# Four banks for the transposes of the first batch, five loads cut at 98 partitions, and one score bank masked by GpSimd

## The chip, the cores and the metric

The kernel runs on one core of a Trainium2 chip. Five engines take part, each with its own queue of instructions that it works through in order: TensorE (PE in the profile) multiplies matrices, VectorE (DVE), ScalarE (ACT) and GpSimd (POOL) work elementwise, and SyncE (SP) issues the transfers between memory and the on-chip buffers. They wait for each other by semaphores. Sixteen DMA engines move the bytes. TensorE writes its results into eight banks of PSUM, each 128 partitions of 512 float32 values; the other engines copy them out.

The metric is device time in microseconds, the median of several runs. A profile shows one execution: its span runs from the first to the last recorded instruction, and its device time is a little longer.

## The reference

Two layers follow each other, for four batches, 8 heads, 768 positions and heads of 48 columns.

```python
state = 0                                       # per batch and head, 48 x 48
for t in range(768):
    state = alpha[:, :, t, :, None] * state + outer(k[:, :, t], v[:, :, t])
    y[:, :, t] = q[:, :, t] @ state
x = y with the heads side by side               # batch, 768, 384
h = relu(x^T @ w_tok1) @ w_tok2                 # mixes the 768 positions, 256 wide
u = x + h^T
out = u + relu(u @ w_ch1) @ w_ch2               # mixes the 384 columns, 1536 wide
```

The first layer is a linear attention with a decay per column, the second a mixer with a token part and a channel part. Inputs and outputs are float32.

## The kernel before, in words

The recurrence is cut into chunks of 128 positions. Inside a chunk the decay is taken out by prefix sums of log alpha: ScalarE takes the logarithm (`la`, line 243), TensorE sums it with a triangular matrix (`cum`), ScalarE takes the exponentials of the sum with both signs (`ek`, `eq`, lines 256 and 258), and k and q are multiplied by them (`pkk`, `pkq`, line 275). TensorE transposes both, multiplies them to scores (`gt`, line 521 in the first batch), a mask keeps the causal half of the scores (`gm`, line 309), and the masked scores times v, together with the state so far, give y (`y`, `inter`), which is copied to `x` (line 333). The state itself goes from chunk to chunk (`state`, `id`, `ss`).

The chunks of batch 0 are worked in three pairs of chunks (256 positions, even and odd positions apart). For a pair there are two transposes of k and two of q, each of four 128x128 blocks. Before the change, one bank holds both transposes of k and another both transposes of q (line 472). Two copies empty each bank, one for each half: `tpk` (line 479) into `tk`, `tpq` (line 481) into `tq`. The half of `tpk` is the half of one transpose. The half of `tpq` takes columns of both transposes, since it interleaves even and odd positions again. Copies of one bank by two engines are ordered one behind the other. The score product of a pair comes in two parts (one for each s), each into two banks, and reads half of `tk` and all of `tq`.

The mixer of batch 0 follows: token products (`tok1`, line 582, one for each chunk and half of w_tok1), `ht` (line 589 or 591), then `xt` and `uT` (lines 629 and 634) that put u transposed into banks, copies `ut` (line 640), and the two channel products `ch1` (line 691, a relu copy `rt` behind each) and `ch2` (line 715, an output copy `o`, line 725 or 728, behind the last). The channel products of a batch are far more work on TensorE than the rest, and they are laid between the chunks of the next batches.

Loads come by SP in the order of the string `LOADS`: `a0 k0 q0 a1 k1 q1 a2 v0 k2 q2 v1 v2 t0 t1 t2 t3 m0 m1`. The letters a, k, q, v with a number are the inputs of one pair of chunks of batch 0 (384 KB). t0 and t1 are the halves of w_tok1, t2 and t3 those of w_tok2 (384 KB each), m0 and m1 the halves of w_ch1 (1152 KB each). n0 to n3, quarters of w_ch2 (576 KB each), come among the loads of batch 1 (string `SECOND`). All weights arrive in float32 and are cast to bf16 (`cast`, lines 756 and 762). Each transfer signals one of eight semaphores in turn, and SP issues the ninth when the first has landed.

The order of the work is written out by hand in the string `ORDER`: every token is one operation by its number in the list `g.ops`, with the engine that does it where there is a choice (A, D or P for ScalarE, VectorE or GpSimd) and, behind the point, the banks that it opens. `f3` is a fill: a matmul on zeros into bank 3 (line 792), which computes nothing that is used. Every engine gets its operations in this order. Nothing at run time changes it.

Of the kernel before, what the change touches and what calls it, by code (L numbers as in the profile page):

```python
# [17 lines left out]
FUSE = 99  # L18
FETCH, BLOCK, AHEAD, ARRIVES = 193, 256, 449, (4.5, 30.0, 3.0)
# [6 lines left out]
0 1 f0 2 f0 f0 f0 f0 f0 3 f0 f0 f0 f0 f0 4 28 f0 29 f0 f0 30.0 5 31.1 32 f2 f2 38 6 f2 35 f2 33 f2 f2 f2 39 f2 34 f2  # L26
36 40 f2 43.2 41 7 f3 66 47.3 f4 65 48 44 49A 50D f4 67.4 46A 45D 68.5 69 f6 51.67 75 72 54.01 8 70 52 f3 f3 76 f3 73
f3 77 f3 80.3 78 f2 9 84.2 56 f6 85 105 81 71 f6 104 87D f6 f6 10 86A f6 f6 83D 106.6 82A 55 107.5 108 53 91.14 11 114
88.23 92 f0 42P 37A f0 f0 109 90 f0 58.07 115 89 57.13 60A 93 f2 116 12 f2 f2 59 f2 f2 f2 112 f2 111 63 61 117 14
123.2 64A f0 62 f0 124 74A 79P 119.0 110 16 120 125D 126A f4 94.41 122A 121D 18 96 127.57 97 130.36 95.20 128 113A  # L30
118P 100 132 98 102 133.4 99A 20 131 13P f5 103A 169.5 101 163.6 24 166.2 f3 15P 129 141.3 135 142.0 143 136 134.17
17P 137 139 145 138D 147 140A 144 146 259 148 150 149 151 19D 152 172.4 178.1 162A 161D 175.7 f0 173 176 174A 167 177D
260 164 168A 170 22D 21P 165A 179 f0 171A 23D f0 261 f0 180A f0 189.0 201.3 190A 195.4 262 202A 181.7 27D 25P 196A
185.2 26D 182A 153 193.6 186A 211.5 264 194D 223.1 263 212D 227.0 224A 265.3 228A 266.4 155 267 217.7 273 270 207.2
274 209.6 268 300 208D 218A 276 213.5 210D 215.1 214A 269 187.0 301 271 216A 203.4 188A 219.3 275 204A 302 225.2 220A
154D 199.7 272 226A 278.65 277 279 200A 303 221.1 280D 281A 156P 183.0 222A 282 283 184A 292.43 284D 285A 197.2 304
294 286.71 157 305 198D 289.05 205.6 287 306.4 288 206A 159 191.2 308 291 307.7 309 311 239.6 296 314 343 290 315
249.1 297 192D 293.54 344 312 319.37 298 295A 345 254.0 316 299A 234.2 158A 346 317 244.5 347 310 313 160D 240 318 348
245 351 241 349 320 352.4 242A 321D 246 322A 354 235 247D 353 350 358 236 356 243 323 362 324 237D 333.64 357 325A
326D 376.5 238 363.2 335 250 248 355 364 336 486 365 327.37 251 487 329 366 367 330.62 328 252A 488 255 332 368 256  # L40
339 369 359.73 331 257A 370.12 340 229.4 361A 360D 253 372D 371A 377 373.60 258 510 334.73 375 489 381.21 341 490 374
337 230 342A 378 382 338A 491 379.5 383 231 380A 492 384.0 232D 511.6 385A 493 513 388.3 512 516 233 386.2 389A 514
517 494 521 495 515 387D 522.7 390.1 496 523 398.5 391 524 394.4 526 396.0 399 392.6 395 400.3 527 535.2 393 518.17
401 497 402.54 528 519A 397 529.63 525 403A 553.1 404D 498 520A 536 405.05 530A 416.4 499 554 406A 440.7 407D 555 531A
500 417D 420.2 539 434.6 421D 441A 501 532.10 435A 550.53 534 422.4 502 430.2 551 546 423A 540.7 533 431A 452.6 558
552 442.0 541 537.5 453D 503 542 438.4 544 538D 559.2 439A 556.1 443D 504 560 543 412.3 545 557D 561 426.6 413D 505
432.7 564 427A 410.5 506 433A 446.4 562 411A 565 408.0 507 447A 563 572.1 577 450.2 409D 508 454.3 573 451A 547.67 574
455D 566.54 509 548A 578.0 549D 591.1 568A 567D 448.2 720 592 580 424.3 584 449D 579 588.76 583 721 425A 569.54 590
418.1 596 582 436.2 570 419A 414.0 571 437A 581 597.3 593 589 722 610.6 575.5 598 444.1 415D 599 601 723 576A 594.2
611 445A 481.4 595D 602 724 744 428.7 476.0 600 429A 725 603 604.35 612 585.61 605A 726 466.2 587D 586A 477 727 606A  # L50
482 728 607.73 751 615.16 609 483 729 755 616 471.5 608 478 617 613.3 730 479 472 614A 484 618.1 480 762 456.7 619D
473 485 773 622.6 731 474 732 620.0 623A 475 457 621A 733 458 734 634.3 459 630.4 735 628.1 635 632.5 631 624.6 780
460 626.0 629 461.7 625 792 736 627 462 737 633 463 636.34 738 464 639.16 637A 467 638D 640A 641D 465 468 799 774.0
469 745.5 775 793.7 656.4 746 778 747 756.3 470 650.6 795 739 757 749 684.1 651D 740 758 644.2 685D 776 748 662.5 794
760 645D 741 660.6 811 663D 657A 678.3 750 742 661D 787.0 769.1 679A 812.7 770 759 668.2 743 777 813 761 672.5 788 814
664.4 669A 673D 789 670.6 665A 666.3 779 671A 646.1 830 667D 682.0 798 647A 831.7 683A 806.2 781.54 797 832 807 763.63
833 752.10 765D 658.2 783A 835 754D 764A 674.7 753D 659D 782A 686.3 808 675D 800.40 687A 803.16 796 802D 816 784.25
801A 766.73 804 680.0 768 818 654.4 681A 836 767 648.1 655A 844.3 786 642.0 649A 817 771.7 785 822.41 643A 652.5 772A
805 834 837 790.2 824 815 653A 809.0 791A 823 838.76 810A 819.51 825.2 839D 820A 828.4 840D 676.0 821A 826 715.7 829D
827 677A 849.65 841.21 845 716 843 846 700.4 851 695.0 850 696 842 852.3 688.1 853D 847.5 689A 705.6 848D 697 854.2  # L60
698 699 717 855A 710.3 718 711 701 719 702 856.1 703 704 712 857A 690.5 713 858.0 714 868.2 859 862.7 860.4 869 864.1
863 866.3 691 861 867 692 865 706 693 873.02 694 870.74 874A 875D 707 871D 872A 910.3 708 894.1 911A 709 880.5 895A
908.2 881D 906.0 909A 912.7 907A 900.4 913A 876.6 901A 896.3 877A 918.1 897A 914.5 919D 904.2 915A 922.0 905D 902.7
923D 920.4 903A 898.6 921A 916.3 899A 888.1 917A 890.5 889A 884.2 891D 878.0 885A 886.7 879A 882.4 887A 892.6 883D
929.3 893A 939.1 930 931 940 932 944.5 933 945 946 934.2 947 941 948 924.0 942 925 943 926 935 927 936 928 949.7 937
950 938 951 954.4 955 952 956 953 957 958
# [12 lines left out]
class Graph:  # L79
# [5 lines left out]
    def add(self, name, costs, emit, reads=(), writes=(), prio=0, dma=None, new=(), tail=0.0, rows=False, loose=False, n=0, late=0.0):  # L85
        self.ops.append(Op(costs, emit, new))
        return self.ops[-1]
# [6 lines left out]
def kernel(  # L94
# [12 lines left out]
    nc = tc.nc  # L107
# [73 lines left out]
    gm_t = many("gm", 2 * NG, [128, 4, 128])  # L181
    ss_t = many("ss", NSS, [128, H, D])
    x_t = many("x", NX, [128, HD])
    ht_t = many("ht", 2 * NDT, [128, HD])
# [19 lines left out]
    def load_input(dst, src, service, keys, prio, loose=False):  # L204
        return g.add("load", {"SP": 0.06}, lambda e: nc.sync.dma_start(dst, src), writes=keys, prio=prio, dma=service, loose=loose)  # L205
# [629 lines left out]
```

## Time and profile before

| | |
|---|---|
| device time, median of 3 runs | 174.05 us (174.0 to 175.09) |
| device time of the profiled execution | 174.24 us |
| its span | 172.5 us |
| TensorE busy | 166.5 us (96%) |
| VectorE busy | 102.0 us (59%) |
| ScalarE busy | 96.0 us (56%) |
| GpSimd busy | 72.3 us (42%) |
| fills of line 792 | 61, 15.1 us |
| loads and stores | 30.2 MB, 175 GB/s over the span |
| granted TensorE clock | 1.00 throughout |

TensorE's busy time counts matmuls that overlap as one stretch, and it counts the fills: a busy TensorE is not always one that does useful work. The lines of the profile have the form start, duration, engine, line, operation, output <- inputs. A bracket at the end tells how long the engine sat idle before it and what it waited for. Tile names leave numbers out: `bank` is any of the eight banks.

### The profile page before, as it was taken

What the parts mean: (1) busy time and instruction counts of PE and PEld (TensorE: products, weight loads), DVE (VectorE), ACT (ScalarE), POOL (GpSimd) and SP (SyncE); (2) the same over time, 40 slices, a digit from 0 to 9 for tenths busy, and PEclk for the clock granted to TensorE, in tenths of its full rate; (3) what the DMA queues carried; (4) which work ended last, traced back from release to release, by engine and by line L of the source; (5) the groups of instructions that cost most, each with busy time, mean ns of one, the idle gap of its engine ahead of it and who ended that gap; (6) DMA issues with size and microseconds to landing.
All of it is one profiled execution on the core that took longest, in us unless ns stands there. A gap on an engine that the chain in (4) does not pass through costs nothing.

```text
span 172.5 us, 5143 instructions
## 1 busy us (share of the span) xinstructions
PE 166.5 (96%) x2099; PEld 106.8 (62%) x2099; DVE 102.0 (59%) x212; ACT 96.0 (56%) x206; POOL 72.3 (42%) x114
## 2 busy tenths in 40 slices
PE   7999979999999999999999999999999999999993
PEld 3566656665666567566666665666676656656562
DVE  3159977544653597689593727495988248132231
ACT  2577552699865655497887231699771112865000
POOL 7252542319485782944877111499941000000000
PEclk9999999999999999999999999999999999999999
DMA  5999999999998999999999999995000221100133
GB/s 134 261 261 265 232 335 398 309 234 337 256 307 168 205 254 219 225 170 198 165 204 151 196 219 223 211 210 92 4 4 0 79 104 50 46 4 0 46 115 113
DMA packets 86150, 30.20 MB, mean 175 GB/s; under 512 B 79600, under 2 KB 85104, under 8 KB 86128
## 3 DMA queue, kind: packets, MB, share of 16 engines
q1 hardware_dynamic: 86128, 29.89, 75.2%
q8 instruction: 16, 0.26, 0.7%
q14 instruction: 6, 0.05, 0.1%
HBM read 25.17 MB, written 4.72 MB: 173 GB/s over the span
## 4 chain that ended last, share of the span: by engine, by line
PE 78%; DVE 6%; POOL 4%; DMA 3%; issue 3%; ACT 2%; SPq 1%; DVEq 0%; POOLq 0%
PE bank L691 27%; PE bank L715 23%; PE bank L289 4%; PE bank L651 3%; DMA ina<-in_alpha_dram 3%; PE bank L602 3%; DVE gm L309 2%; PE bank L387 2%; PE bank L338 2%; PE bank L423 2%; POOL pkk L275 2%; PE bank L521 1%; PE bank L411 1%; PE bank L352 1%; SPq L205 1%
## 5 line engine op out<-in xcount | busy, mean ns | idle before, releaser
L691 PE MATMUL bank<-ut,wc 128*128 128x384 bf16 x288 | 51.1, 326 | 0.0
L691 PEld LDWEIGHTS <-wc 128*128 128x128 bf16 x288 | 26.6, 98 | 16.5
L275 POOL TENSOR_TENSOR pkk<-ink,ek 128x384 bf16<-128x384 f32 x24 | 24.3, 1022 | 17.7 <-ACT ek L256 14.9
L715 PE MATMUL bank<-wc,rt 128*128 128x384 bf16 x144 | 26.5, 326 | 0.0
L715 PE MATMUL bank<-wc,rt_late 128*128 128x384 bf16 (+2 forms) x156 | 25.1, 314 | 0.0
L728 DVE TENSOR_TENSOR o<-bank,x 128x384 f32<-128x384 f32 (+2 forms) x19 | 10.1, 536 | 18.2 <-PE bank L715 18.2
L589 ACT ACTIVATE rt<-bank 128x384 bf16<-128x384 f32 x33 | 16.3, 494 | 7.4 <-PE bank L691 7.0
L282 POOL CAST vb<-inv 128x384 bf16<-128x384 f32 x21 | 10.5, 506 | 22.3 <-DMA inv<-in_v_dram 17.6
L715 PEld LDWEIGHTS <-rt_late 128*128 128x128 bf16 x156 | 14.4, 98 | 8.2
L275 POOL TENSOR_TENSOR pkq<-inq,eq 128x384 bf16<-128x384 f32 x18 | 17.9, 1003 | 2.8 <-ACT eq L258 2.8
L589 ACT ACTIVATE rt_late<-bank 128x384 bf16<-128x384 f32 x33 | 16.1, 495 | 5.3 <-PE bank L691 5.3
L309 DVE TENSOR_TENSOR gm<-bank,u 128x512 bf16<-128x512 f32 x28 | 17.3, 682 | 2.8 <-PE bank L387 2.6
L243 ACT ACTIVATE la<-ina 128x384 bf16<-128x384 f32 x24 | 12.1, 526 | 10.8 <-DMA ina<-in_alpha_dram 10.8
L715 PEld LDWEIGHTS <-rt 128*128 128x128 bf16 x144 | 13.2, 98 | 7.7
L792 PE MATMUL bank<-zeros 128*128 128x384 bf16 x61 | 15.1, 372 | 1.4 <-DVE la L192 1.2
L591 DVE TENSOR_SCALAR rt_late<-bank 128x384 bf16<-128x384 f32 x15 | 8.3, 554 | 10.0 <-PE bank L691 8.3
L309 DVE TENSOR_TENSOR gm<-bank,pmask 128x512 bf16<-128x512 f32 x20 | 12.7, 682 | 1.4 <-PE bank L521 1.3
L256 ACT ACTIVATE ek<-bank 128x384 f32<-128x384 f32 x24 | 11.4, 498 | 3.5 <-PE bank L355 2.0
L333 ACT CAST x<-bank 128x384 bf16<-128x384 f32 x16 | 7.3, 483 | 10.6 <-PE bank L338 9.4
L322 POOL TENSOR_TENSOR ss<-st,al 128x384 bf16<-128x384 f32 x12 | 10.0, 832 | 7.4 <-DVE st L319 5.4
L591 DVE TENSOR_SCALAR rt<-bank 128x384 bf16<-128x384 f32 x15 | 7.9, 554 | 5.3 <-PE bank L691 5.3
L297 ACT COPY tkq<-bank 128x512 bf16<-128x512 bf16 x17 | 9.3, 602 | 2.8 <-PE bank L289 2.7
(118 smaller groups left out, 237.3 us busy)
## 6 DMA issues: line engine op xcount, KB each, us to landing
out_dram<-o SPq DMA_DIRECT2D x23, 192.0 KB, 2.6
ina<-in_alpha_dram SPq DMA_DIRECT2D x14, 192.0 KB, 4.3
ink<-in_k_dram SPq DMA_DIRECT2D x14, 192.0 KB, 4.6
inq<-in_q_dram SPq DMA_DIRECT2D x14, 192.0 KB, 4.5
inv<-in_v_dram SPq DMA_DIRECT2D x14, 192.0 KB, 4.4
rt_late<-in_moe_w_ch_dram SPq DMA_DIRECT2D x2, 1152.0 KB, 10.1
rt_late<-in_moe_w_ch_dram SPq DMA_DIRECT2D x4, 576.0 KB, 7.1
ina<-in_alpha_dram SPq DMA_DIRECT2D x5, 384.0 KB, 6.3
```

What stands on the lines that cost most here:

```text
L243: g.add("la", {"ACT": 0.43}, lambda e: act.activation(la[:, :, 0:D], t, AF.Ln), key, [u["la"][1]], pr + 5)
L256: g.add("ek", {"ACT": 0.38}, lambda e: act.activation(ek, banks[bank.place][:, 0:HD], AF.Exp, scale=-1.0), [bank], [kek], pr + 4)
L275: lambda e, dst=dst, src=src, ex=ex: {"POOL": gps, "DVE": dve}[e].tensor_tensor(dst[:, :, 0:D], src, ex().rearrange("p (h d) -> p h d", h= ...
L282: lambda e: evict[e](vb, src), ksrc, [u["vb"][1]], pr + 4)
L309: g.add("gm", {"DVE": 0.60}, lambda e: dve.tensor_tensor(gm, banks[bank.place].rearrange("p (j t) -> p j t", j=4), wide(mask, [[0, 4], lis ...
L322: g.add("ss", {"POOL": 0.79}, lambda e: gps.tensor_tensor(ss, st.rearrange("p (h d) -> p h d", h=H), wide(al, [[1, 8], [0, D]]), ALU.mult) ...
L589: act.activation(dst, src, AF.Relu)
L591: dve.tensor_scalar_max(dst, src, 0.0)
L691: pe.matmul(banks[bank.place][:, 0:HD], lhsT=wc1[wp][:, kc, off : off + 128], rhs=ut_t[b % 2][:, kc, cs], start=(kc == 0), stop=(kc == NM ...
L715: pe.matmul(banks[bank.place][:, 0 : hi - lo], lhsT=rt_t[(b * NDC + mc) % NRT][:, i * 128 : i * 128 + 128], rhs=wc2[:, mc, lo:hi], start=( ...
L728: g.add("o", {"DVE": 0.09 + 0.38 * width}, lambda e, i=i, bank=bank, o=o, lo=lo, hi=hi: dve.tensor_tensor(o[:, lo:hi], banks[bank.place][: ...
L792: pe.matmul(banks[place][:, 0:HD], lhsT=zeros[:, 0:128], rhs=zeros, start=True, stop=True, skip_group_check=True)
```

## The change

1. For batch 0's pairs, the transposes of k get two banks, one for each s, and those of q two banks, one for each half that a copy takes out. So a pair's transposes lie in four banks and every copy reads a bank of its own.
2. Five loads, v0, v2, t3, n1 and n3, are issued as two transfers, of the first 98 partitions and of the other 30. They fill the same tile.
3. For one bank of scores (pair 2, counted from 0, s = 1, the odd heads) the mask on VectorE is replaced by a copy to bf16 on ScalarE (`raw`, into a new tile `sc`) and a masked product on GpSimd (`gmp`). By this one operation more, all later operations have a number higher by one.
4. `ORDER` is new throughout: which engine does a copy or cast, which bank an operation gets, and where it stands. It has 57 fills instead of 61. In the opening, ScalarE has four casts of weights (t0, t2, a third of m0, and another later) where it had one.

A split of the product y (`SPLIT`) is written too but is empty, so y stays as it was.

```diff
+UNEVEN = "v0 v2 t3 n1 n3".split()
+SPLIT, AROUND = (), ((2, 1, 1),)
...
-    def load_input(dst, src, service, keys, prio, loose=False):
-        return g.add("load", {"SP": 0.06}, lambda e: nc.sync.dma_start(dst, src), ...)
+    def load_input(dst, src, service, keys, prio, loose=False, uneven=False):
+        def emit(e):
+            for rows in (slice(0, 98), slice(98, 128)) if uneven else (slice(0, 128),):
+                nc.sync.dma_start(dst[rows], src[rows])
+
+        op = g.add("load", {"SP": 0.12 if uneven else 0.06}, emit, ...)
...
+        if around:
+            raw = sc_t[slot % 2]
+            g.add("raw", {"ACT": 0.48}, lambda e: act.copy(raw, banks[bank.place].rearrange("p (j t) -> p j t", j=4)),
+                  [bank], [("raw", slot % 2)], prio)
+            g.add("gmp", {"POOL": 1.15}, lambda e: gps.tensor_tensor(
+                gm, raw, wide(mask, [[0, 4], list(mask.ap[1])]), ALU.mult), [("raw", slot % 2)], [("gm", slot)], prio)
+            return
...
-                bank = Bank()
+                tb = [Bank(), Bank()]
...
-                        ps = banks[bank.place].bitcast(BF16)
                         for j in range(4):
-                            pe.transpose(ps[:, 512 * s + 128 * j :][:, 0:128], src[:, 2 * j : 2 * j + 2, :], id128)
+                            part, at = (s, 128 * j) if w == "k" else (j // 2, 256 * s + j % 2 * 128)
+                            pe.transpose(banks[tb[part].place].bitcast(BF16)[:, at : at + 128], src[:, 2 * j : 2 * j + 2, :], id128)
...
-                            evict[e](tk2[:, part], ps[:, 512 * part : 512 * part + 512].rearrange("p (j t) -> p j t", j=4))
+                            evict[e](tk2[:, part], ps[:, 0:512].rearrange("p (j t) -> p j t", j=4))
                         else:
                             evict[e](tq2[:, 2 * part : 2 * part + 2].rearrange("p j (t s) -> p (j t) s", s=2),
-                                     wide(ps[:, 256 * part : 256 * part + 1], [[1, 256], [512, 2]]))
+                                     wide(ps[:, 0:1], [[1, 256], [256, 2]]))
...
-                s_mask(gb[par], pmask[s], 2 * i + par, pr + 1)
+                s_mask(gb[par], pmask[s], 2 * i + par, pr + 1, b == 0 and (sc, s, par) in AROUND)
```

The numbers in braces are costs that an earlier planner used; nothing reads them when the kernel runs.

More of the change, by code (lines that the diff above doesn't have):

```diff
@@ L31 @@
[L31 to L40, printed above, removed]
@@ L83, in __init__, with add @@
         self.ops = []
-    def add(self, name, costs, emit, reads=(), writes=(), prio=0, dma=None, new=(), tail=0.0, rows=False, loose=False, n=0, late=0.0):
+    def add(self, name, costs, emit, reads=(), writes=(), prio=0, dma=None, new=(), tail=0.0, rows=False, loose=False, n=0, late=0.0, banks=(), gates=()):
         self.ops.append(Op(costs, emit, new))
@@ L305, in s_transpose, with s_mask @@
         s_transposed(n, tb, dst, key, prio)
-    def s_mask(bank, mask, slot, prio):
+    def s_mask(bank, mask, slot, prio, around=False):
         gm = gm_t[slot]
+        if around:
[5 more added lines that the diff above has]
+            return
         g.add("gm", {"DVE": 0.60}, lambda e: dve.tensor_tensor(
@@ L547, in paired_chunks, with within @@
         g.add("state", {"PE": 0.34 if last else 0.44}, kv, [us[0]["pk"][1], us[1]["pk"][1], *kvb], sbk, pr + 1, new=sbk, rows=True, n=16)
-        def within(e):
+        def within(e, parts):
             for h in range(H):
-                for s in both:
+                for s in parts:
                     for c in both:
@@ L557, in within @@
                                   stop=(sc == 0 and c == 0 and s == 1), skip_group_check=True)
-        g.add("y", {"PE": 0.52}, within, [*kgm, *kvb], yb, pr + 1, new=yb, rows=True, n=32)
+        for parts in ((0,), (1,)) if (b, sc) in SPLIT else (both,):
+            g.add("y", {"PE": 0.26 * len(parts)}, lambda e, parts=parts: within(e, parts),
+                  [k for s in parts for k in (*kgm[2 * s : 2 * s + 2], kvb[s])], yb, pr + 1, new=yb if 0 in parts else [], rows=True,
+                  n=16 * len(parts))
         for c in both:
@@ L759, in weight @@
             dst, key = wc2[:, NM * i : NM * i + NM, :], ("wc2", i)
-            op = load_input(staged, src, 1.55, keys, 2000, loose)
+            op = load_input(staged, src, 1.55, keys, 2000, loose, f"{which}{i}" in UNEVEN)
             costs, prio = {"POOL": 1.2, "ACT": 1.15, "DVE": 0.75}, 1310
```

94 lines of the change are left out of this document (54 added, 40 removed).

## The prediction

> **What bounds the kernel now.** I read the head of the page, then busy time by stretch, then the fill matmuls of line 792 alone, then the timeline where the first channel matmul stands.
>
> ```profile
> span 172.5 us, 5143 instructions
> ```
>
> ```profile
> 16.00:20.00 4.00, 3.88 (x97) 2.56 (x96) 3.88 (x8) 2.56 (x8) 1.60 (x2) 1.00 1.14 245
> 20.00:24.00 4.00, 2.88 (x70) 2.13 (x72) 2.78 (x8) 2.33 (x5) 1.61 (x4) 1.00 1.00 301
> 28.00:33.00 5.00, 4.92 (x39) 3.12 (x37) 3.07 (x6) 2.95 (x7) 0.83 (x1) 1.00 1.07 368
> 33.00:56.00 23.00, 23.00 (x283) 14.35 (x282) 11.71 (x19) 17.92 (x39) 13.51 (x17) 1.00 1.03 259
> 56.00:60.00 4.00, 3.92 (x69) 2.36 (x71) 2.21 (x5) 2.80 (x7) 2.88 (x5) 1.00 1.04 190
> 60.00:110.00 50.00, 49.68 (x699) 31.94 (x692) 34.99 (x68) 29.47 (x64) 24.82 (x38) 1.00 1.06 205
> ```
>
> ```profile
> 8.00:33.00 25.00, 9.22 (x42) 3.55 (x39) 1.00 1.12 303
> 33.00:172.50 139.50, 0.09 (x1) 0.00 (x0) 1.00 0.69 151
> ```
>
> ```profile
> 32.92 1.30 PE L691 MATMUL bank<-ut,wc 128*128 128x384 bf16 x7
> ```
>
> The columns of the stretches are length, then busy time of TensorE, weight loads, VectorE, ScalarE and GpSimd, the granted clock, the DMA share and GB/s. Before 33 us TensorE looks busy, but 42 matmuls of that stretch are fills on zeros. Behind it there is practically no fill and no gap: 23.00 of 23.00 us, then 49.68 of 50.00. So the kernel has two parts. From the first channel matmul (line 691, 32.92 us) to the end lie 172.5 - 32.92 = 139.6 us of TensorE work and a tail. Ahead of it lies an opening that waits.
>
> Counted in the two written orders, exactly the same TensorE operations stand ahead of the first channel matmul before and after (12 token products, 6 prefix sums, 12 transposes, 6 score products and so on), with 61 fills before and 57 after, and none later in either. So the change is worth the shift of that one instant, plus or minus gaps that appear later. The device time of the profiled run was 174.24 us: its span and 1.74 us around it.
>
> What holds the opening, from the chain that ended last and from the waits between 8 and 33 us:
>
> ```profile
> 21.17 0.61 DVE tq L481
> 21.80 0.59 ACT tq L481
> 22.39 0.50 ACT tk L479
> 22.91 0.44 DVE tk L479
> 23.35 0.04 issue
> 23.39 0.64 PE bank L521 x32
> ```
>
> ```profile
> DVE tq L481 <- ACT tq L481: 1.4, 1, 1.4
> ...
> DVE tk L479 <- ACT tk L479: 1.1, 1, 1.1
> ```
>
> VectorE is full from 16 to 20 us (3.88 of 4.00), mostly with masks. And where it is not full it takes turns: the two halves of a transposed tile lie in one bank, and the second engine starts when the first is done. For the third pair four copies stand one behind another, 21.17 to 23.35, and the score product waits for the last. Then the loads take over:
>
> ```profile
> 20.80 0.50 POOL L282 CAST vb<-inv 128x384 bf16<-128x384 f32 x1 [0.44 <-DMA inv<-in_v_dram]
> 22.66 0.51 POOL L282 CAST vb<-inv 128x384 bf16<-128x384 f32 x1 [1.35 <-DMA inv<-in_v_dram]
> 23.77 0.83 POOL L762 CAST wt<-ina 128x768 bf16<-128x768 f32 x1 [0.60 <-DMA ina<-in_moe_w_tok_dram]
> 25.30 0.83 POOL L762 CAST wt<-ink 128x768 bf16<-128x768 f32 x1 [0.70 <-DMA ink<-in_moe_w_tok_dram]
> 26.28 0.83 POOL L762 CAST wt<-inq 128x768 bf16<-128x768 f32 x1 [0.15 <-DMA inq<-in_moe_w_tok_dram]
> 30.73 0.83 POOL L756 CAST wc<-rt_late 128x768 bf16<-128x768 f32 x1 [3.63 <-DMA rt_late<-in_moe_w_ch_dram]
> ```
>
> ```profile
> 31.18 0.56 DVE L640 CAST ut<-bank 128x384 bf16<-128x384 f32 x1 [1.16 <-PE bank L634]
> 31.65 1.02 DVE L756 CAST wc<-rt_late 128x768 bf16<-128x768 f32 x2
> ```
>
> These are GpSimd's casts of loads, then VectorE's two rows ahead of the first channel matmul; the bracket tells the idle time ahead and what ended it. v1 lands at 20.8, v2 at 22.65, the parts t0, t1 and t2 of the token weights at 23.8, 25.3 and 26.3, and m0, the first half of w_ch1, at 30.7: GpSimd stood 3.63 us for it.
>
> **Part 1, four banks.** Pair 3: the four copies in a row cost 23.35 - 21.17 = 2.2 us. With halves in banks of their own VectorE does 0.61 + 0.44 = 1.05 and ScalarE 0.59 + 0.50 = 1.09 beside each other, so 1.1 us less. Of the waits above, the 1.1 is VectorE's in this pair and the 1.4 its own in pair 1; that one bounds what pair 1 can gain from above, and nothing bounds it from below, where the transposes come last. I take 0.5 us for pair 1 and for pair 2 each. The number of transposes is the same; only their places in banks differ. That each tile now holds two banks costs the order, not an engine: a bank is reused after its reader, and no engine waits for a bank in the opening today by the waits listed.
>
> **Part 2, the mask behind a copy.** VectorE loses one of its 12 masks of the opening; the first row below has the masks of all such pairs.
>
> ```profile
> L309 DVE TENSOR_TENSOR gm<-bank,pmask 128x512 bf16<-128x512 f32 x20 | 12.7, 682 | 1.4 <-PE bank L521 1.3
> ...
> L322 POOL TENSOR_TENSOR ss<-st,al 128x384 bf16<-128x384 f32 x12 | 10.0, 832 | 7.4 <-DVE st L319 5.4
> ```
>
> A mask takes 0.68 us, which is the gain there. ScalarE pays about 0.59 (its 128x512 copy above). GpSimd's masked product of 512 has no row: from below 0.83 (384 elements), from above 0.83 x 512 / 384 = 1.11, and I take 1.11. Fed by pair 3's score product (21.7 below) and the copy, it is done by 21.7 + 0.3 + 0.6 + 1.1 = 23.7, ahead of the weight cast behind it on GpSimd, whose load lands at 25.3. So it is hidden; were t1 down at 23, it would cost the cast 0.7.
>
> **Part 3, the new order.** On VectorE the masks of pair 1 no longer stand behind those of pair 2, the first state product is fed earlier (it waits for v0 alone, not for VectorE), and casts of the opening move: t0, t2 and a third of m0 onto ScalarE, while t3 on VectorE now stands ahead of the last x copy. Walking it: a1's load and the copies behind it are as now, so pair 1's score product comes 0.5 us earlier (part 1) and VectorE starts on masks near 11.4. It has four masks, two pkq products of 384 columns (0.56, as the ut copy of that width) and a tq copy to do, 4 x 0.68 + 2 x 0.56 + 0.61 = 4.5, and is ready for pair 2's score product near 15.9; two masks and a state product (1.9) end near 17.9. Then it is out of work until q2 lands, and loads decide. With q2 at 18.1 (part 4) two pkq products, a mask, a state product, a mask and a copy take 3.6, and pair 3's score product comes near 21.7, against 23.39; with q2 at 19.4, near 23.0. The casts in ScalarE's queue have x and ut copies behind them: those now wait for t0, t2 and m0 to land, where GpSimd's casts had nothing urgent behind them.
>
> **Part 4, the split loads.** SP issues each of v0, v2, t3, n1, n3 twice. It keeps eight transfers in flight and waits with the ninth for the first; with v0 as two, k2's issue waits for k0 instead of a0, both down long before its turn at 10.2, and the issues themselves run ahead of the landings by 6 to 8 us, so what they add is hidden. What is to be had shows in two loads of equal size and the 2.5 us between them:
>
> ```profile
> L205 SPq DMA_DIRECT2D inv<-in_v_dram x1: 1440/1440/1440, 8.7 to 8.7; - x1
> ...
> DMA to landing us min/median/max: 6.3/6.3/6.3
> ```
>
> ```profile
> L205 SPq DMA_DIRECT2D ink<-in_k_dram x1: 1389/1389/1389, 10.2 to 10.2; - x1
> ...
> DMA to landing us min/median/max: 7.7/7.7/7.7
> ```
>
> ```profile
> q8 instruction: 1, 0.02, 3.1%
> ```
>
> The first is v0 (8.74 to 15.0), the second k2, the next issue (10.23 to 17.9). Between 14 and 16.5 us one 16 KB instruction packet took 3.1% of 16 engines x 2.5 us = 1.24 us. One packet of 1.24 us sits on one DMA engine, and k2 landed 2.9 us behind v0 where the issues of this stretch stand 1.44 us apart: some 1.4 us late for everybody, because one engine is. 98 = 14 x 7 and 30 = 15 x 2: dealt over the most engines that divide them, 14 engines get 9 rows of 128, one gets 2 and one none, where each has 8 today. From below (the engine that fetches is one of the two relieved): k2, q2 and v1 come 1.44 - 0.18 = 1.25 us earlier, where 0.18 = 1.44 / 8 is the ninth row of the others. From above (it is one of the 14): each split load costs 0.18, so v0, v2 and t3 make 0.5 us later. No row of before says which engine fetches. I take the lower end for the first fetch (it is the nearer to the rows: one engine late by 1.4, one relieved of 1.44), and for m0, where loads run at 368 GB/s and all engines share that, only half a microsecond: 30.2 instead of 30.7.
>
> [...]
>
> **The sum.** t3 stands about 0.9 behind t2 (as t2 behind t1), less the relief: an estimate of 26.7. Its cast (0.51), the last x copy (0.56) behind it on VectorE, the last token products and a ht copy (1.2, estimated) lead to the uT products near 29.0, which last 2.2 (12 matmuls at 1.30 / 7): over by 31.2, the first ones far earlier. So m0 decides. Behind it at 30.2 VectorE casts its third (0.51) and copies two ut tiles that the first channel matmul needs (0.56 each), and the matmul stands at 30.2 + 1.6 = 31.8. Now it is 32.92, 2.2 us behind m0, because the casts stand behind a ut copy and two of them on VectorE. So 32.92 - 31.8 = 1.1 us less, and with later gaps as now 174.24 - 1.1 = 173.1. The median of the runs is 0.2 lower than the profiled one: 172.9.
>
> **Rivals.** *Loads come clear of the fetches altogether (172.0).* If relief counts for every load ahead of m0 and not for the first ones alone, m0 at 29.7, a full microsecond early, puts the channel matmul at 31.35, 1.6 us less, and the 0.4 us of gaps behind 56 us (0.08 up to 60, 0.32 up to 110) close: 174.24 - 2.0 = 172.2, less 0.2. For it: five loads are split ahead of 57 us. Against it: at 368 GB/s around m0 shifting rows moves no byte away.
>
> *The split does nothing (174.1).* All engines share what binds, m0 stays at 30.7 with 0.36 of ninth rows, and the shorter cast chain (1.6 for 2.2) is eaten: 32.7, a gain of 0.2. [...]
>
> *Slower: the fetching engine is one of the 14 (175.7).*
>
> ```profile
> 57.12 0.51 POOL L282 CAST vb<-inv 128x384 bf16<-128x384 f32 x1 [3.20 <-DMA inv<-in_v_dram]
> ```
>
> ```profile
> 58.65 0.34 PE L411 MATMUL bank<-vb,pkk 128*128 128x96 bf16 x4
> ```
>
> m0 lands at 31.2, so the channel matmul keeps its 32.9. The two rows are from 57 to 59 us, GpSimd's and TensorE's. At 57.1 a v load already gates GpSimd, and the product on line 411 goes 1.5 us behind it. With five ninth rows (0.18, 0.18, 0.18, and half as much again for the larger n1 and n3) it lands 1.1 us later, and the new order has one group of four channel matmuls (4 x 1.30 / 7 = 0.74) less ahead of that product: TensorE stands up to 1.7 us, 174.24 + 1.7 - 0.2 = 175.7. It decides from where the landing passes 57.1.
>
> **How the numbers follow.** Forecast 0.42 (172.4 to 173.7 on its own), loads clear 0.28, nothing 0.12, slower 0.18. The range 171.6 to 175.6 leaves the ends of the second and fourth. One per cent, 1.74 us, is about what a measurement of this kernel tells from no change: faster by more is the second case and the edge of the first, 0.35; slower by more is most of the fourth, 0.14; the rest 0.51.
>
> **What would show it.** Right: no copy of tq or tk waits for the other engine's; k2's load lands in about 6.5 us; pair 3's score product at 21.6; m0's cast at 30.2; first L691 matmul at 31.8; TensorE full behind it. Wrong: landings as late as now, ScalarE idle ahead of its weight casts with x or ut copies behind them, or TensorE waiting near 57 us for a state product.

## The result, and the profile after

| | before | after |
|---|---|---|
| device time, median | 174.57 us (174.0 to 175.11) | 182.3 us (181.02 to 183.44) |
| device time and span of the profiled execution | 174.24, 172.5 us | 181.02, 179.3 us |
| first channel matmul | 32.92 us | 34.41 us |

Both medians are of four runs; the table ahead of the prediction has three of those of before. One run of `e2_before_split` below is in a slower state and is left out of its time and ratio. The ratio is 1.0441, with a 95% interval of 1.0356 to 1.0527: the change makes the kernel slower by 4.4%. The forecast was 172.9 us.

First the busy time by stretch of the kernel after; the columns are as in the prediction (length, then busy time of TensorE, weight loads, VectorE, ScalarE, GpSimd, then granted clock, DMA share, GB/s).

```profile
32.00:48.00 16.00, 15.83 (x149) 9.35 (x147) 7.29 (x14) 12.04 (x26) 8.14 (x10) 1.00 1.06 258
48.00:50.00 2.00, 0.71 (x5) 0.30 (x3) 1.63 (x3) 0.58 (x2) 0.00 (x0) 1.00 0.86 209
50.00:52.00 2.00, 1.53 (x44) 1.14 (x44) 2.00 (x5) 1.78 (x5) 0.83 (x1) 0.88 0.98 230
52.00:54.00 2.00, 2.00 (x12) 1.16 (x11) 1.51 (x3) 1.58 (x4) 1.56 (x3) 0.50 1.13 346
54.00:56.00 2.00, 2.00 (x44) 1.25 (x43) 0.00 (x0) 0.13 (x1) 2.00 (x3) 0.76 1.02 238
56.00:64.00 8.00, 7.06 (x96) 4.41 (x94) 2.65 (x5) 4.16 (x8) 3.75 (x6) 1.00 1.06 171
```

The same view of the kernel before, for the stretches that answer to them:

```profile
32.00:48.00 16.00, 16.00 (x182) 9.77 (x181) 8.94 (x16) 14.44 (x32) 7.77 (x9) 1.00 1.06 271
48.00:64.00 16.00, 15.93 (x247) 9.92 (x245) 9.35 (x18) 9.17 (x20) 12.46 (x18) 1.00 1.02 234
```

The span grew by 6.8 us, and three places hold most of it. The channel work starts 34.41 - 32.92 = 1.5 us later. TensorE then stands 0.17 + 1.29 + 0.47 + 0.94 = 2.9 us up to 64 us, where before it stood 0.07. And from 50 to 56 us its granted clock is 0.88, 0.50 and 0.76, which loses about 2 x (0.12 + 0.50 + 0.24) = 1.7 us (an estimate, as if TensorE had had work all the time). Together 6.0 of the 6.8.

What held TensorE stands in the chain that ended last of the kernel after (start, duration, engine, line), and in three of ScalarE's rows:

```profile
39.34 8.94 DMA rt_late<-in_moe_w_ch_dram
...
48.37 0.09 DVE wc L782
...
49.59 0.60 DVE tq L525
...
51.19 8.21 DMA rt_late<-in_moe_w_ch_dram
59.49 0.06 DVE wc L782
...
60.16 0.43 DVE tk L522
60.60 0.32 PE bank L368
```

```profile
49.42 0.52 ACT L252 ACTIVATE la<-ina 128x384 bf16<-128x384 f32 x1 [2.43 <-DMA ina<-in_alpha_dram]
49.85 0.57 ACT L525 COPY tq<-bank 128x512 bf16<-128x512 bf16 x1
60.03 0.52 ACT L252 ACTIVATE la<-ina 128x384 bf16<-128x384 f32 x1 [2.03 <-DMA ina<-in_alpha_dram]
```

The two transfers are the second pieces of the cut loads n1 and n3. VectorE waits for each to cast it (2.01 us up to 48.37, 2.78 up to 59.49), and behind that cast in its queue stand the copies `tq` and `tk` of the next chunk, which TensorE needs. ScalarE stands in the same two stretches for a load of alpha. Those loads are whole, but SP issues them right behind the cut ones, and they land late too. In the first wait ScalarE's half of `tq` ends last, at 50.42 us (VectorE's ends at 50.19); in the second `la` and `tk` end together, at 60.55 and 60.58. So it is not the cut loads alone that TensorE waits for, but the whole row of loads from them on. The opening is late in the same way; GpSimd's casts of the loads (and its masked product):

```profile
21.82 0.50 POOL L291 CAST vb<-inv 128x384 bf16<-128x384 f32 x1 [1.33 <-DMA inv<-in_v_dram]
24.13 0.51 POOL L291 CAST vb<-inv 128x384 bf16<-128x384 f32 x1 [1.80 <-DMA inv<-in_v_dram]
25.16 1.15 POOL L322 TENSOR_TENSOR gm<-sc,pmask 128x512 bf16<-128x512 bf16 x1 [0.53 <-ACT sc L320]
33.13 1.22 POOL L776 CAST wc<-rt_late 128x768 bf16<-128x768 f32 x1 [5.82 <-DMA rt_late<-in_moe_w_ch_dram]
```

v1 is cast at 21.8 (before: 20.8), v2 at 24.1 (22.7), m0 at 33.1 (30.7). So loads are the suspect, and the experiments take the change apart there first.

### The profile page after: what moved, and what is told of

Its sections match the earlier page's. It is cut to its first block, busy times and chain, and to the rows that moved or that the text cites. A ratio compares the mean times of both kernels' runs of the same rounds, so it can differ in the third digit from the quotient of the medians.

```text
span 179.3 us, 5162 instructions
## 1 busy us (share of the span) xinstructions
PE 168.8 (94%) x2095; PEld 107.0 (60%) x2095; DVE 99.6 (56%) x209; ACT 99.3 (55%) x210; POOL 71.6 (40%) x114
## 4 chain that ended last, share of the span: by engine, by line
PE 63%; DMA 20%; SPq 9%; DVE 3%; issue 1%; POOL 1%; DVEq 0%
PE bank L735 24%; PE bank L711 20%; DMA rt_late<-in_moe_w_ch_dram 17%; SPq L210 9%; DMA inv<-in_v_dram 4%; PE bank L622 3%; PE bank L298 3%; PE bank L671 3%; PE bank L403 2%; PE bank L439 2%; PE bank L368 2%; PE bank L354 1%; POOL wc L776 1%; PE bank L427 1%; DVE x L677 1%
## 5 line engine op out<-in xcount | busy, mean ns | idle before, releaser
L735 PE MATMUL bank<-wc,rt 128*128 128x384 bf16 x144 | 28.1, 335 | 0.0
L609 ACT ACTIVATE rt_late<-bank 128x384 bf16<-128x384 f32 x38 | 18.5, 493 | 9.2 <-PE bank L711 8.9
L325 DVE TENSOR_TENSOR gm<-bank,u 128x512 bf16<-128x512 f32 x28 | 17.9, 684 | 3.6 <-PE bank L403 3.5
L291 POOL CAST vb<-inv 128x384 bf16<-128x384 f32 x22 | 11.0, 507 | 19.8 <-DMA inv<-in_v_dram 14.9
L609 ACT ACTIVATE rt<-bank 128x384 bf16<-128x384 f32 x31 | 15.2, 496 | 2.6 <-PE bank L711 2.5
L812 PE MATMUL bank<-zeros 128*128 128x384 bf16 x57 | 14.1, 375 | 1.2 <-DVE la L195 1.2
L349 ACT CAST x<-bank 128x384 bf16<-128x384 f32 x14 | 6.5, 479 | 14.0 <-PE bank L354 11.6
L611 DVE TENSOR_SCALAR rt<-bank 128x384 bf16<-128x384 f32 x17 | 9.3, 555 | 6.1 <-PE bank L711 6.0
L611 DVE TENSOR_SCALAR rt_late<-bank 128x384 bf16<-128x384 f32 x10 | 5.5, 554 | 10.0 <-ACT rt_late L609 6.1
```

Source lines behind the costliest of these rows:

```text
L291: lambda e: evict[e](vb, src), ksrc, [u["vb"][1]], pr + 4)
L325: g.add("gm", {"DVE": 0.60}, lambda e: dve.tensor_tensor(gm, banks[bank.place].rearrange("p (j t) -> p j t", j=4), wide(mask, [[0, 4], lis ...
L609: act.activation(dst, src, AF.Relu)
L611: dve.tensor_scalar_max(dst, src, 0.0)
L735: pe.matmul(banks[bank.place][:, 0 : hi - lo], lhsT=rt_t[(b * NDC + mc) % NRT][:, i * 128 : i * 128 + 128], rhs=wc2[:, mc, lo:hi], start=( ...
L812: pe.matmul(banks[place][:, 0:HD], lhsT=zeros[:, 0:128], rhs=zeros, start=True, stop=True, skip_group_check=True)
```

## The parts alone

The first runs tell Theory A (the cut loads lose the time) from Theory B (the new order, banks and mask do). In `e1_whole` all loads are whole, in `e2_before_split` the kernel before has the five loads cut and nothing else.

```diff
 e1_whole, from the changed kernel:
-UNEVEN = "v0 v2 t3 n1 n3".split()
+UNEVEN = ()
 e2_before_split, from the kernel before:
+UNEVEN = "v0 v2 t3 n1 n3".split()
...
+            for rows in (slice(0, 98), slice(98, 128)) if uneven else (slice(0, 128),):
+                nc.sync.dma_start(dst[rows], src[rows])
...
```

> The changed kernel with its five split loads issued whole again; order, banks and the GpSimd mask stay. Theory A (the split transfers lose the time: v0 in two parts landed at 16.2 us instead of 15.0, m0 at 33.1 instead of 30.7): loads land as in the kernel before, m0 at 30.7, first channel matmul near 32.3, and the whole at 173.5 us, 172 to 175. Theory B (the new order loses it, since it hangs ScalarE's copies behind weight casts and puts less channel work ahead of the waits at 48 to 60 us): 178 to 182.

> The kernel before, its order untouched, with v0, v2, t3, n1 and n3 issued as 98 and 30 partitions. Theory A: v0 lands near 16.1 us, m0 near 33, and the time goes up by 4 to 8 us, to 178 to 182. Theory B: within 1.5 us of the kernel before, 173 to 175.5.

`e1_whole`: 174.68 us, ratio 1.0028 (0.9979 to 1.0077). `e2_before_split`: 179.96 us, ratio 1.0293 (1.0232 to 1.0354). Theory B falls as a cause of its own: order, banks and mask together make no measurable difference, and cutting the loads alone makes the old order slower too. But the old order loses 2.9% by the cut and the new one 4.4%, so the new order is the more sensitive to late loads; no run tells which part of it is.

Two more cut the same five loads at other rows, since 98 and 30 were chosen for the number of engines that divides them.

```diff
 e3_split64:
-            for rows in (slice(0, 98), slice(98, 128)) if uneven else (slice(0, 128),):
+            for rows in (slice(0, 64), slice(64, 128)) if uneven else (slice(0, 128),):
 e4_split112:
+            for rows in (slice(0, 112), slice(112, 128)) if uneven else (slice(0, 128),):
```

> The changed kernel with the same five loads cut at 64 and 64 partitions, so both parts have a row count that 16 divides. If it is the number of transfers (eight in flight, two completions) that costs, v0 lands as late as in the changed kernel (16.2 us) and the time is 180 to 183 us. If it is the dealing of 98 and 30 rows over 14 and 15 engines, v0 lands near 15.1 and the time is 173 to 176.

> The changed kernel with the five loads cut at 112 and 16 partitions: sixteen engines for both parts, 7 rows and 1 row each, so no engine has more rows than in a whole load, but a row lies on another engine than in a load of 128. If the fewer engines and the ninth row are the price, v0 lands near 15.1 us and the time is 173 to 176. If it is the place of the rows (a row moves slower when the engines walk the partitions in runs of seven), v0 lands 0.3 to 0.8 us later than whole and the time is 177 to 182.

`e3_split64`: 182.92 us, ratio 1.0506 (1.0445 to 1.0567). `e4_split112`: 180.0 us, ratio 1.0326 (1.0271 to 1.038). How the kernel after deals 98 and 30 rows shows in the landings of v0's pieces: of the 98 rows one at 10.52 us, just behind the issue, and 14 from 14.88 to 15.64; of the 30 one just behind the issue too (11.79), one at 13.85 and 14 from 15.52 to 16.22. The loads of 128 rows ahead of them have 16 landings close together (a2: 13.16 to 14.13). 64, 112 and 16 rows divide by sixteen as 128 does, and if they are dealt in equal shares like it (an inference), neither the ninth row on 14 engines nor an engine that is left out is needed for the loss: both cuts lose.

## What the cut costs

Theory T: each further transfer costs some 0.6 us at its end. Theory P: a transfer that writes only some of the partitions moves its packets more slowly. The busy time by stretch while v0 moves separates them; the last two columns are DMA share and GB/s. With whole loads (`e1_whole`):

```profile
13.00:14.00 1.00, 1.00 (x13) 0.61 (x11) 1.00 (x4) 1.00 (x3) 0.23 (x1) 1.00 1.26 260
14.00:15.00 1.00, 1.00 (x14) 0.74 (x12) 1.00 (x2) 1.00 (x3) 0.04 (x1) 1.00 1.27 269
```

The kernel after, with 98 and 30 rows:

```profile
13.00:14.00 1.00, 1.00 (x10) 0.57 (x9) 1.00 (x4) 0.58 (x1) 0.71 (x1) 1.00 1.27 209
14.00:15.00 1.00, 1.00 (x16) 0.89 (x16) 1.00 (x3) 0.85 (x4) 0.00 (x0) 1.00 1.36 215
15.00:16.00 1.00, 1.00 (x15) 0.64 (x14) 1.00 (x3) 1.00 (x4) 0.00 (x0) 1.00 1.20 192
```

The engines are as busy as ever and move a fifth to over a quarter less. That is slow packets, not pauses. (In every run one 16 KB packet of instructions starts between 13.7 and 15.0 us, at 14.95 in the kernel before and at 14.53 in the kernel after; the row of one us in which it starts reads 16 GB/s high.) Four runs then vary how the loads are cut.

```diff
 e5_free (all 128 partitions in both transfers; t3 by columns):
...
+                half = (dst.shape[1] + 1) // 2
+                nc.sync.dma_start(dst[:, 0:half], src[:, 0:half])
+                nc.sync.dma_start(dst[:, half:], src[:, half:])
 e6_alternate:
+            for rows in (slice(0, 128, 2), slice(1, 128, 2)) if uneven else (slice(0, 128),):
 e7_v0_quarters:
+UNEVEN = ["v0"]
+            for rows in [slice(32 * x, 32 * x + 32) for x in range(4)] if uneven else (slice(0, 128),):
 e8_opening:
+UNEVEN = "v0 v2 t3".split()
```

> The changed kernel with the same five loads as two transfers each, but cut inside the rows: every transfer has all 128 partitions, with the rows' packets of 384 and 1536 bytes as before (the cut of t3 alone makes 3072 byte rows into 1536). Theory P (a transfer that writes only some of the partitions moves its packets more slowly; the queue stays busy): in the loads cut by rows DMA engines stayed at a share of 1.2 to 1.36 and moved 190 to 215 GB/s from 13 to 15 us, where the whole loads moved 260 to 270 at the same share. With all partitions in each transfer the rate stays at 255 to 270 from 13 to 17 us, v0 lands at 14.8 to 15.1, the first channel matmul starts at 32.0 to 32.6, and the time is that of the whole loads, 174.7 us (173.5 to 176). Theory T (each further transfer costs some 0.6 us at its end, whatever it holds): the rate falls with the share of busy engines, v0 lands at 15.5 or later, the first channel matmul starts at 34 or later, 180 to 183 us.

> The changed kernel with the five loads as two transfers of 64 partitions each, every other partition in one and the rest in the other, so that each transfer writes over the whole height of the tile. Theory P, by place (neighbouring partitions share a way in, and a transfer of 64 in a row uses half of the ways): no loss, 255 to 270 GB/s from 13 to 16 us, v0 at 14.8 to 15.1, 174 to 176.5 us. Theory P, by count (fewer partitions, wherever they are, are slower): like the halves in a row, 190 to 215 GB/s at a share of 1.3, v0 at 15.5, 181 to 184 us. Theory T: the same 181 to 184 us, with a lower share.

> The changed kernel with all loads whole but v0, which is four transfers of 32 partitions in a row. Theory P: half as many partitions as in the halves, about half of their rate: 90 to 130 GB/s while v0 moves, at a share of 1.2 or more; v0's 384 KB take 3 to 4.2 us where they took 1.5, so that it lands at 16.5 to 17.6, and everything behind it is 1.8 to 2.7 us later. Theory T: three further transfers at 0.65 us, v0 at 16.7 to 17, with a share under 1 in the gaps and packets as short as before. Time by either: the opening alone is 1.8 to 2.7 us late, 176 to 178.5 us if later loads catch up none of it.

> The changed kernel with v0, v2 and t3 as 98 and 30 partitions, and n1 and n3 whole. If the loss is that of the opening (m0 2.2 us later than with whole loads, first channel matmul at 34.4 where it was 32.2), most of it stays: 178 to 180.5 us, with TensorE's holes at 24 to 32 us and shorter ones at 48 to 60. If the loss comes from n1 and n3, whose late pieces hold back the loads behind them until TensorE stands at 48 to 64 us: 175 to 177.

| run | time, us | ratio to before |
|---|---|---|
| `e5_free` | 174.97 | 1.0012 (0.9971 to 1.0053) |
| `e6_alternate` | 174.86 | 1.0007 (0.9974 to 1.0039) |
| `e7_v0_quarters` | 175.3 | 1.0046 (1.0014 to 1.0077) |
| `e8_opening` | 176.93 | 1.0144 (1.0065 to 1.0223) |

The same view of `e6_alternate`, then of `e7_v0_quarters`:

```profile
13.00:14.00 1.00, 1.00 (x13) 0.57 (x11) 1.00 (x4) 0.88 (x2) 0.43 (x1) 1.00 1.28 262
14.00:15.00 1.00, 1.00 (x14) 0.76 (x12) 1.00 (x3) 1.00 (x4) 0.00 (x0) 1.00 1.27 268
```

```profile
13.00:14.00 1.00, 1.00 (x10) 0.57 (x9) 1.00 (x4) 0.58 (x2) 0.73 (x1) 1.00 1.34 191
14.00:15.00 1.00, 1.00 (x16) 0.90 (x16) 1.00 (x3) 1.00 (x4) 0.00 (x0) 1.00 1.35 215
```

Theory T falls: ten transfers in place of five cost nothing if each has all partitions (`e5_free`) or every other one (`e6_alternate`). Theory P holds by place: 64 partitions spread over the tile are fast (262 and 268 GB/s), 64 in a row are slow (190 and 215 in `e3_split64`). But its size was missed in `e7_v0_quarters`: 32 in a row are no slower than 64, 191 and 215 GB/s where 90 to 130 were expected, and 175.3 us where 176 to 178.5 were.

`e8_opening` has the late start of its first expectation (first channel matmul at 34.55 us) and nearly the time of its second (176.93 us, 175 to 177 expected): TensorE stands only 0.43 us from 32 to 64 us. So most of what the three loads of the opening cost (1.4%, 2.5 us) is the later start, 34.55 - 32.92 = 1.6 us; the long waits behind 48 us come with n1 and n3.

Two runs then ask which side is slow, the memory that is read or the tile that is written. Only v0 is cut, and its rows go to other partitions than they should.

```diff
 e9_halves_written:
+            to = (slice(0, 64), slice(64, 128)) if uneven else (slice(0, 128),)
+            of = (slice(0, 128, 2), slice(1, 128, 2)) if uneven else (slice(0, 128),)
+            for x, y in zip(to, of):
+                nc.sync.dma_start(dst[x], src[y])
 e10_halves_read: the lists of to and of exchanged
```

> All loads whole but v0, which is two transfers: each writes 64 partitions in a row and reads every other row of the source. (Rows of v0 so stand in the wrong partitions: the output is another; the work is the same.) If it is the writing that makes neighbours slow: 190 to 215 GB/s from 13 to 15 us at a share of 1.3, as with halves in a row on both sides. If it is the reading (rows next to each other in memory): 255 to 270.

> The other way round: each of v0's two transfers reads 64 rows in a row and writes every other partition (the output is another, the work is the same). If the writing decides: 255 to 270 GB/s from 13 to 15 us, as with whole loads. If the reading decides: 190 to 215. If both runs lose a part, both sides count.

`e9_halves_written`, then `e10_halves_read`, the same view:

```profile
13.00:14.00 1.00, 1.00 (x12) 0.57 (x10) 1.00 (x4) 0.59 (x1) 0.46 (x1) 1.00 1.33 184
14.00:15.00 1.00, 1.00 (x13) 0.68 (x11) 1.00 (x3) 0.98 (x3) 0.00 (x0) 1.00 1.37 211
```

```profile
13.00:14.00 1.00, 1.00 (x11) 0.57 (x10) 1.00 (x4) 0.64 (x2) 0.66 (x1) 1.00 1.35 276
14.00:15.00 1.00, 1.00 (x15) 0.89 (x14) 1.00 (x3) 1.00 (x3) 0.00 (x0) 1.00 1.18 255
```

The writing decides. The reading costs nothing, in a row or not. These are single runs, at 174.24 and 174.46 us: a slow v0 alone hardly moves the time (0.5% in `e7_v0_quarters`), so here and below the rates and landings of v0 decide, and not the times.

32 partitions in a row move as fast as 64, so their number does not set the rate. Their place in the tile might: the next run moves 64 in a row as the halves do, but from the middle of the tile, 32 to 95.

```diff
 e13_middle:
+UNEVEN = ["v0"]
+            for rows in (slice(32, 96), slice(0, 32), slice(96, 128)) if uneven else (slice(0, 128),):
```

> All loads whole but v0, which is three transfers: partitions 32 to 95 first, then 0 to 31, then 96 to 127. The first is 64 partitions in a row, as the slow halves are, but from the middle of the tile. Rival 1 (neighbours are slow, wherever they stand): 175 to 215 GB/s through the whole of v0, from 13.2 to 15 us, as with the halves. [...]

`e13_middle`, the same view in quarter microseconds, and below it `e3_split64`, where v0 is two halves in a row:

```profile
13.25:13.50 0.25, 0.25 (x4) 0.10 (x1) 0.25 (x1) 0.25 (x1) 0.18 (x1) 1.00 1.27 261
13.50:13.75 0.25, 0.25 (x4) 0.10 (x3) 0.25 (x3) 0.25 (x2) 0.00 (x0) 1.00 1.63 325
13.75:14.00 0.25, 0.25 (x6) 0.25 (x6) 0.25 (x1) 0.25 (x1) 0.00 (x0) 1.00 1.32 187
14.00:14.25 0.25, 0.25 (x6) 0.21 (x4) 0.25 (x2) 0.25 (x2) 0.00 (x0) 1.00 1.23 148
```

```profile
13.25:13.50 0.25, 0.25 (x7) 0.25 (x7) 0.25 (x1) 0.01 (x1) 0.00 (x0) 1.00 1.31 178
13.50:13.75 0.25, 0.25 (x7) 0.21 (x5) 0.25 (x2) 0.00 (x0) 0.00 (x0) 1.00 1.39 181
```

The packet of instructions falls into the second quarter of `e13_middle`; the DMA view of that quarter (packets, MB, share of 16 engines):

```profile
q8 instruction: 1, 0.02, 34.9%
```

Its 16 KB are 65 of the 325 GB/s there, so the load itself moved at 260. 64 partitions in a row from the middle move at 261 and 260 GB/s, 64 from the edge at 178 and 181, and the outer 32s at 187 and 148 (191 from 14 to 15 us). So Rival 1, neighbours as such, falls by the rates. The slow pieces of 32 and 64 rows, halves and quarters, each lie in one half of the tile; those that move at the whole load's rate, 32 to 95 here and every other row in `e6_alternate`, reach into both. Why that counts, no run shows. By its landings v0 ended some 0.5 us late, so the three pieces together were no faster than two halves. The rates of this one run carry the argument.

By the landings in the trace, v0 took 1.5 us after a2 with whole loads, every other row and reading in halves, 1.9 with 112 and 16, 2.0 to 2.2 in halves and quarters, 2.1 to 2.3 in 98 and 30 (medians over the engines). In the last two cuts the larger piece is slow as well: the 98 alone took 1.6 to 1.7 us and the 112 took 1.6, where seven rows in place of eight for each engine should take 7/8 of 1.5, 1.3 us (an estimate at the whole load's rate). About half of the loss or more lies in these larger pieces. Why they are slow is open.

## Opening and late loads

`e8_opening` left 3% unexplained, so the two late loads are cut alone.

```diff
 e14_late:
+UNEVEN = "n1 n3".split()
```

> The changed kernel with n1 and n3 as 98 and 30 partitions, and v0, v2 and t3 whole. With the three opening loads alone cut, the time was 1.44 per cent over the kernel before; with all five 4.4 per cent. If the two add up, n1 and n3 alone cost about 3 per cent: 178.5 to 180.5 us, with TensorE standing at 48 to 62 us, and the first channel matmul at 32 to 32.7 as with whole loads. If the late pieces cost much only because the opening is late too (a stretch in which TensorE waits so long that its granted clock falls): 175.5 to 177.5 us, no granted clock under 1.00 from 48 to 64 us.

`e14_late`: 178.09 us, ratio 1.0222 (1.0176 to 1.0269). The busy time where TensorE stands longest, and its longest wait there:

```profile
52.00:56.00 4.00, 2.83 (x33) 1.49 (x31) 0.00 (x0) 1.15 (x1) 1.96 (x4) 1.00 1.02 162
```

```profile
PE bank L368 <- ACT la L252: 2.2, 1, 2.2
```

It lies between the two expectations: two cut loads far from the opening cost 2.2%, the three of the opening 1.4%. The sum, 3.7%, is within the interval of all five (3.6 to 5.3). The clock's 1.7 us in the profile after would be 1.0% more; none of it shows in `e14_late`, whose granted clock stays at 1.00. The other executions agree: over the whole span the four of the kernel after were granted 0.99, 0.99, 0.988 and 0.972 (the last is the slowest, 183.44 us), the four of `e14_late` 0.998 to 1.00. That speaks for the clock as the rest, but no execution with these five cuts in the new order has a full clock, so it is not shown.

## The banks and the mask alone

Both from `e1_whole`, each with one part undone.

```diff
 e11_two_banks (both transposes of a tensor in the bank that opens first):
-                            part, at = (s, 128 * j) if w == "k" else (j // 2, 256 * s + j % 2 * 128)
+                            at = 512 * s + 128 * j
...
 e12_plain_mask:
-            g.add("raw", {"ACT": 0.48}, lambda e: act.copy(raw, banks[bank.place].rearrange("p (j t) -> p j t", j=4)),
+            g.add("raw", {"ACT": 0.48}, lambda e: None,
-            g.add("gmp", {"POOL": 1.15}, lambda e: gps.tensor_tensor(gm, raw, ...
+            g.add("gmp", {"POOL": 1.15}, lambda e: dve.tensor_tensor(gm, banks[bank.place]...
```

> The changed order with whole loads, and both transposes of one tensor in one bank as before, so that the two copies of a tensor out of it follow one another. By the prediction's first part the four banks bring up to 1.1 us to pair 3's score product and half a us to those of pairs 1 and 2. In this order the copies of q for pair 3 ran side by side at 21.48 and 21.86 us: one after the other they end 0.2 to 0.5 us later, so the score product comes at 22.9 to 23.3 (22.66 with four banks), and the first channel matmul at 32.3 to 32.8 (32.2). Time: if the start of the channel matmuls sets the end, 0.2 to 0.6 us more than 174.7; if the loads up to 57 us set it, no difference (174 to 175.5).

> The changed order with whole loads, and the one score bank masked by VectorE straight from the bank, without the copy and without GpSimd. By the prediction the copy and the mask behind it are hidden and bring next to nothing: 174 to 175.5 us, first channel matmul at 32.0 to 32.8. Rival: VectorE's 0.68 us more at 24 us delays the masks behind it, pair 3's last product and all that follows by up to 0.7 us: 175 to 176.

`e11_two_banks`: 174.32 us, ratio 1.0002 (0.9975 to 1.003). `e12_plain_mask`: 174.96 us, ratio 1.0051 (1.0023 to 1.0079). Neither can be told from `e1_whole` (1.0028, 0.9979 to 1.0077). From the timelines, pair 3's score product and the first channel matmul of `e1_whole`, then the same two of `e11_two_banks`:

```profile
22.66 0.42 PE L538 MATMUL bank<-tq,tk 48*64 48x128 bf16 x16
...
32.23 3.75 PE L711 MATMUL bank<-ut,wc 128*128 128x384 bf16 x22 [0.60 <-POOL wc L776]
```

```profile
22.73 0.42 PE L539 MATMUL bank<-tq,tk 48*64 48x128 bf16 x16
...
31.93 4.32 PE L712 MATMUL bank<-ut,wc 128*128 128x384 bf16 x24
```

In this order four banks bring 0.07 us to pair 3, where 0.2 to 0.6 were expected, and the first channel matmul stands at 32.23 with both parts, at 31.93 without the four banks and at 32.52 in `e12_plain_mask`. Profiles differ by more than that for other reasons: pair 1's product, which copies in turn can only delay, starts at 11.10 us in `e1_whole` and at 10.85 in `e11_two_banks`. What taking turns costs pair 3 here is in VectorE's row of `e11_two_banks`, a wait of 0.16 us:

```profile
22.00 0.69 DVE L499 COPY tq<-bank 128x512 bf16<-128x512 bf16 x1 [0.16 <-ACT tq L499]
```

Why does an earlier start of the channel work bring nothing? Busy time by stretch of `e1_whole`, later on, and what TensorE waits for in them:

```profile
32.00:48.00 16.00, 15.49 (x176) 9.40 (x177) 9.75 (x18) 13.12 (x31) 7.92 (x11) 1.00 0.98 256
48.00:64.00 16.00, 14.43 (x215) 8.77 (x217) 7.72 (x14) 8.86 (x18) 11.18 (x16) 1.00 0.94 222
```

```profile
PE bank L368 <- ACT la L252: 1.1, 1, 1.1
PE bank L735 <- ACT wc L782: 0.5, 1, 0.5
```

The matmuls start 32.92 - 32.23 = 0.7 us earlier and TensorE then stands 2.1 us up to 64 us, for work on batch 1's loads and on w_ch2. The `la` of the first wait starts at 55.36 us, when its load of alpha has landed; the same `la` of the kernel before starts at 54.11. So up to there the loads set the pace, and they come no earlier. This profile is of the slowest of the run's four executions (176.12 us), so its 2.1 us are more than usual; but `e11_two_banks`, profiled at 174.71, starts 1.0 us earlier than the kernel before and stands 0.95 us in the same stretch. No run was faster than the kernel before.

## Why the prediction was wrong

- **The step that failed is part 4's price of a split load.** It had two ends, 1.25 us earlier for the loads behind the first fetch and 0.18 later for each split. Both counted rows per engine and took an engine's rate as given wherever its rows go. Measured, v0 alone landed 0.4 to 0.8 us later in each way of cutting it into pieces in a row, since its packets slowed (by the microsecond from 13 to 15 us 184 to 215 GB/s in halves, quarters and 98 and 30, 222 and 234 with 112 and 16, where whole loads moved 260 to 269) while the engines stayed busy. The rows themselves went over the engines as part 4 has it, by the landings of 98 and 30 rows above. The slowing holds for equal shares too, where the price by rows is nothing.
- **The relief did not come.** k2's sixteen landings in the trace had one straggler before (17.90 us, the others by 16.48) and have one after (18.38, the others by 17.48), while two others land early (15.71 and 16.12). So the engine that fetches was not among the relieved here. That was the condition of the rival on the slower side, which came nearest: its mechanism, late loads behind 57 us at which TensorE stands, is what the chain after shows, at 48 as well as 60 us. Its price, 1.7 us, left out the slower packets, the later opening and the clock; and the 1.1 + 0.74 that it names add up to 1.8.
- **"The split does nothing"** stands in the prediction at 174.1; its own terms, 174.24 - 0.2 - 0.2, give 173.8. Two transfers for one cost nothing here if both reach over the tile's whole height (ratios 1.0012 in `e5_free`, 1.0007 in `e6_alternate`), but two halves in a row cost 5.1% (`e3_split64`).
- **The sum** said "with later gaps as now". `e1_whole` shows that this fails even without the cut: 0.7 us earlier, then 2.1 us of standing. m0, at 30.2 in the sum, was cast at 33.1 with the cut loads and at 30.9 with whole ones, so nothing brought it forward. The chain from m0's landing to the channel matmul was 1.6 us in the sum and is 34.41 - 33.13 = 1.3 in the profile after.
- **Part 1** had the mechanism: no copy of tq or tk in the opening waits for the other engine's any more; the waits after name only TensorE ahead of them. Its size, 1.1 us for pair 3, was wrong: 0.07. The new order itself puts both `tk` copies on ScalarE ahead of the `tq` copies (at 19.35 and 21.00 us in `e1_whole`), so only the two `tq` copies were left to take turns, 0.16 us. Part 3's other branch, pair 3 near 23.0 if q2 comes at 19.4, is close to the 22.66 of `e1_whole`. But that row is half of pair 3's product, and the other half stands at 23.94, behind the 23.39 at which the whole stood before. Its 15.9 for pair 2 is met in the same way, for the first half (15.89 us; the second is at 17.51).
- **Part 2** was right: GpSimd's masked product took 1.15 us (row above; 1.11 taken), ScalarE's copy 0.58, and both are hidden: in `e12_plain_mask`, without them, the time is the same within the noise.

## What to carry to other kernels

Before a load is cut, ask which partitions each piece writes, not only how many rows each engine gets: pieces spread over the tile's whole height cost nothing here, pieces of 32 or 64 rows within one half of it moved at 184 to 215 GB/s where whole loads moved 260 to 269, some 70 to 80% of the rate; the 98 and the 112 rows took 1.6 to 1.7 us where their count alone gives 1.3. A cast that waits for a load holds everything behind it in its engine's queue, so a late load is paid by whatever stands there, and by whatever waits for the loads issued behind it. And an earlier start of the main work is worth nothing while loads set the pace behind it: look for the last load that gates it before pricing the opening.

## What was not expected of the hardware

- 32 partitions in a row are written as fast as 64 in a row (191 GB/s from 13 to 14 us in `e7_v0_quarters`, against 190 in `e3_split64`), and 64 from the middle of the tile as fast as 128 (261 and 260 GB/s in `e13_middle`, against 260 in `e1_whole`).
- In the kernel after, TensorE's wait of 1.76 us ahead of 50.47 us was followed by a granted clock of 0.50 from 52 to 54 us. In `e14_late` a wait of 2.2 us was followed by none. `e3_split64` has both in one trace: the clock stayed at 1.00 behind a wait of 2.2 us at 48 to 50 us, and fell to 0.53 from 60 to 62 us behind one of 1.9.

```profile
50.47 0.64 PE L538 MATMUL bank<-tq,tk 48*64 48x128 bf16 x32 [1.76 <-ACT tq L525]
```

So the length of the wait alone does not tell whether the clock falls behind it. What else decides it, no run shows.
